# An attention-and-MLP kernel: some probability tiles turned on TensorE instead of by DMA, new numbers in the planner's table, and two rounds of planning

## The chip, the cores and the metric

The kernel runs on one NeuronCore of one Trainium2 chip. The metric is device time in microseconds (us), from launch to end; a profiled execution also has a span, from its first to its last instruction. Lower is better.

The engines are called by the names that the profile uses: PE (TensorE matmuls; PEld is its weight load), DVE (VectorE), ACT (ScalarE), POOL (GpSimd) and SP (SyncE, whose queue issues every DMA here).

## The reference

Attention over 4 batches of 8 heads, 576 tokens, 64 values a head, with scores below (row maximum minus tau) dropped, and then two MLPs over the 2304 rows that it gives.

```python
scores = scale * np.matmul(q, k.transpose(0, 1, 3, 2))
thresh = np.max(scores, axis=-1, keepdims=True) - tau
scores = np.where(scores >= thresh, scores, -1000000000.0)
attn = np.exp(scores - np.max(scores, axis=-1, keepdims=True))
attn = attn / (np.sum(attn, axis=-1, keepdims=True) + 1e-09)
x = heads_side_by_side(np.matmul(attn, v))          # 2304 x 512
x = (s * np.maximum(x @ w_in, 0) ** 2 + b) @ w_out  # 512 -> 2048 -> 512
h = x @ w2_in
out = (h / (1 + np.exp(-1.702 * h))) @ w2_out
```

## The kernel before

Nothing is issued in the order of the code. Every piece of work is handed to a `Plan` as a step with the engines that may do it, an estimated cost on each, what it reads and writes, and an urgency (`prio`). `Plan.run` lays all steps out in simulated time, on each engine the most urgent ready step first, and the kernel is then emitted in that order. Each engine works its own list strictly in that order, so a step that waits holds up all that stands behind it on its engine. The table `KN` holds the planner's numbers: `t0` to `t4` are the times from which the MLP's passes take their urgencies, `boost`, `lead` and `ahead` move attention, weight loads and weight conversions against them.

**Attention.** The heads go in 16 pairs, four to a batch, and each pair has nine score tiles of 128 rows by 576 keys, 144 tiles in all (`tile_step`). One tile runs like this: PE writes the scores S into PSUM; DVE takes the row maximum `nm` (L511), then two one-column values from it, `nb` (L522) and the threshold `tb` (L516); ACT does the exponential e (L529); DVE multiplies by the threshold mask and sums (L533, called the product below); ACT makes a half-precision copy `p` (L324), POOL the rest that the copy lost (L542 and L543); and a transposing DMA on SP's queue puts both into `PT`, `PTm` for the tile that both heads share (L545). When a pair's nine tiles are through, PE multiplies `PT` with the values V (L605, L646). Tiles named `gt`, `xa`, `xb`, `acca` and `accb` are lent to attention while the MLP does not use them yet. S has two PSUM buffers and one lent; the PSUM tag T has one and one lent, and serves V's scales, the reciprocals, and the results of L605 and L646.

**V's scales** (`prep_v`) take a reduction, six small DVE instructions (L447, L448, L449, each once for either head) and a reciprocal.

**Weights.** They arrive as 8-byte numbers in 64 blocks and are converted to 4-byte floats (`convert`): two ACT instructions (L732, L757), three on DVE (`ww` L738, `wa` L742, `wh` or `ww` L749) and a POOL addition (L759); the result is also stored.

**MLP.** Rows go in five blocks: four of 512 tokens (xa and xb) and one of 256. `hidden` (L788) multiplies by the first matrix, `project` (L851) by the second, on PE, three products for each because operands are split into a high and a low part; the first block of the first MLP does one full-precision product instead. The first MLP block needs the four pairs of batch 0.

Of the kernel before, what the change touches and what calls it, by code (L numbers as in the profile page):

```python
# [20 lines left out]
P = 128  # L21
# [23 lines left out]
    "spread": 8,  # L45
}

# [22 lines left out]
class Plan:  # L70
# [50 lines left out]
    def run(self, engines):  # L121
        steps = self.steps
        for op in steps:
            op["left"] = len(op["after"])
            for a in op["after"]:
                steps[a]["then"].append(op["n"])
        slots = {k: q[0].bufs for k, q in self.turns.items()}
        next_turn = dict.fromkeys(self.turns, 0)
# [3 lines left out]
        clock = Clock()  # L132
        for seg in range(self.segment + 1):
# [7 lines left out]
            while count < len(todo):  # L141
# [4 lines left out]
                while ends and ends[0][0] <= now:  # L146
                    for b in steps[heapq.heappop(ends)[1]]["bufs"]:
                        b.users -= 1
                        if b.users == 0:
                            slots[id(b.pool), b.tag] += 1  # L150
                moved = False
                for e in engines:
# [3 lines left out]
                    while ready[e]:  # L156
# [12 lines left out]
                        need = {}  # L169
                        ok = True  # L170
                        new = sorted((b for b in op["bufs"] if not b.live), key=lambda b: b.turn)
                        for b in new:
                            k = (id(b.pool), b.tag)
                            i = need.get(k, 0)
                            if b.turn != next_turn[k] + i or slots[k] <= i:
                                ok = False
                                break
                            need[k] = i + 1
                        if not ok:
                            put.append((p, n))  # L180
                            continue
                        for b in new:
                            b.live = True
                        for k, i in need.items():
                            next_turn[k] += i
                            slots[k] -= i
                        op["start"], op["on"] = now, e
# [7 lines left out]
                        if op["queued"]:  # L195
                            moved_at = max(now + op["queued"], moved_at)
                            if op["turns"]:
                                avail[e] = moved_at + 110.0
                            moved_at += lag
                            end = moved_at + 900.0  # L200
                        heapq.heappush(ends, (end + 180.0, n))
# [80 lines left out]
class Kernel:  # L282
# [9 lines left out]
    def consts(self, pool):  # L292
        nc = self.nc
        self.ident = pool.tile([P, P], F32, name="ident")
        make_identity(nc, self.ident)
        sc = pool.tile([P, 3], F32, name="scal")
        for i, src in enumerate((self.tau, self.s, self.b)):
            nc.sync.dma_start(sc[:, i : i + 1], src.partition_broadcast(P))
        self.s_ap, self.b_ap = sc[:, 1:2], sc[:, 2:3]
# [9 lines left out]
        self.under = pool.tile([P, 1], F32, name="under")  # L309
        nc.vector.tensor_tensor(self.under, t1, t2, ALU.add)  # L310
# [44 lines left out]
    def ps(self, tag, shape):  # L355
# [5 lines left out]
        return Buf(self.pa if own else self.px, tag, shape, F32, n if own else more)  # L361
# [55 lines left out]
    def prep_v(self, p):  # L417
# [24 lines left out]

        def scales(_):
            nc.vector.tensor_reduce(vm.ap, T.ap, AX.X, ALU.max)
# [6 lines left out]
        add({"DVE": 1085.0}, scales, [T], [vm, vs, vcol])  # L451
# [11 lines left out]
    def tile_step(self, p, i):  # L463
# [38 lines left out]
        else:  # L502
# [4 lines left out]
        tb = self.at("tb", [P, 1], F32, bufs=4)  # L507
# [3 lines left out]
            {"DVE": 668.0}, lambda _: nc.vector.tensor_reduce(nm.ap, Sv(), AX.XY, ALU.max, negate=True), [Sp], [nm],  # L511
# [6 lines left out]
        )  # L518
        nb = self.at("nb", [P, 1], F32, bufs=4)
        add(  # L520
            {"DVE": 130.0},
            lambda _: nc.vector.tensor_scalar(nb.ap, nm.ap, LOG_SP, None, ALU.add), [nm], [nb],  # L522
            prio=self.plan.prio - KN["tb"] * pace - 1.0,
# [5 lines left out]
            lambda _: nc.scalar.activation(ev(), Sv(), AF.Exp, bias=nb.ap, scale=1.0), [Sp, nb], [e],  # L529
# [4 lines left out]
                ev(), Sv(), tb.ap, ev(), ALU.is_ge, ALU.mult, accum_out=p["acc"][:, i, 0:1]  # L534
            ),
            [Sp, tb, e], [e, (p["acc"], i)], prio=self.plan.prio - KN["sc"] * pace,
# [8 lines left out]
        add({"SP": (1360.0, 1800.0, 1280.0)}, lambda _: nc.sync.dma_start_transpose(pt(), p16.ap), [p16], [(PT, part)], turns=True)  # L545
# [116 lines left out]
    def attention(self, pairs):  # L662
# [3 lines left out]
        for n, p in enumerate(pairs):  # L666
# [8 lines left out]
            if n == 0:  # L675
                do(self.prep_qk, p, 0)
            p["PT"] = {}
# [414 lines left out]
```

## Time and profile before

| | |
|---|---|
| median of 3 runs | 1100.98 us (1099.6 to 1103.26) |
| the profiled execution's own time | 1097.05 us |
| its span | 1095.2 us |
| PE busy | 1034.4 us (94%) |
| DVE busy | 810.4 us (74%) |
| ACT busy | 675.6 us (62%) |
| POOL busy | 430.6 us (39%) |

The profiled execution ran 3.9 us under the median. "Busy" is the time in which an engine had at least one instruction in work; the granted clock of PE is told apart from it, and a busy PE at half the clock does half the work.

### The profile page before, as it was taken

The page shows a single profiled execution, that of the slowest core. Times are in us where ns is not written, and L with a number is a line of the kernel's source. Part 1 is how long each engine was busy: PE and PEld are TensorE (multiplying, and loading weights), DVE is VectorE, ACT ScalarE, POOL GpSimd, SP SyncE. Part 2 cuts the span into 40 slices and gives each one's busy share as a digit, 9 for nine tenths or more (in the row PEclk, how much of TensorE's full clock was granted, in tenths as well). Part 3 has the DMA queues.
Part 4 walks back from the last instruction along what each step waited for, and adds up shares of the span by engine and source line. Part 5 has one row for each costly group of instructions (what it writes and reads, how often), then busy time and mean ns, then how long its engine had stood idle before and what let it go on. Part 6 is the DMA issues. An engine that isn't in the chain of part 4 may idle for free.

```text
span 1095.2 us, 16161 instructions
## 1 busy us (share of the span) xinstructions
PE 1034.4 (94%) x5264; PEld 754.5 (69%) x5264; DVE 810.4 (74%) x1727; ACT 675.6 (62%) x1216; POOL 430.6 (39%) x477
## 2 busy tenths in 40 slices
PE   3777889999999999999999999999999999999998
PEld 1333334445678777878877787868888888888886
DVE  6999798999898988999998878765444544444443
ACT  5776778778988765776666587655655433223221
POOL 2765565757775577556556343500000000000000
PEclk7777899999999998999999999999999999999999
DMA  7999899898988656768576866542211112020102
GB/s 220 202 188 225 217 244 247 211 255 239 227 197 227 165 136 171 204 170 223 139 187 162 198 171 145 127 139 78 78 60 66 30 49 68 1 68 10 54 34 67
DMA packets 228756, 161.54 MB, mean 147 GB/s; under 512 B 180728, under 2 KB 181312, under 8 KB 228672
## 3 DMA queue, kind: packets, MB, share of 16 engines
q1 hardware_dynamic: 228672, 160.52, 57.3%
q8 instruction: 41, 0.67, 0.3%
q14 instruction: 43, 0.35, 0.1%
HBM read 93.85 MB, written 24.15 MB: 108 GB/s over the span
## 4 chain that ended last, share of the span: by engine, by line
PE 56%; DVE 6%; issue 2%; ACT 1%; DMA 1%; SPq 0%; POOL 0%; DVEq 0%; ACTq 0%; POOLq 0%
PE y L851 27%; PE y L788 26%; PE S L490 2%; PE T L605 1%; DVE e L533 1%; DVE ww L749 1%; DVE nm L511 1%; DVE gl L339 1%; DVE ww L738 0%; DVE wl L339 0%; DMA wst<-in_moe_w_in 0%; DVE accb L864 0%; DVE wa L742 0%; DMA raw<-in_q 0%; DVE gt L816 0%
## 5 line engine op out<-in xcount | busy, mean ns | idle before, releaser
L542 POOL TENSOR_TENSOR p<-e,p 128x512 f16<-128x512 f32 x123 | 151.3, 1230 | 150.7 <-ACT p L324 122.1
L788 PE MATMUL y<-xa,wh 128*128 128x512 f32 x512 | 183.8, 453 | 0.0
L788 PE MATMUL y<-xb,wh 128*128 128x512 f32 x512 | 164.0, 401 | 0.4 <-DVE xb L339 0.4
L851 PE MATMUL y<-gh,wh 128*128 128x512 f32 (+1 forms) x384 | 156.1, 449 | 3.3 <-POOL wh L759 2.0
L529 ACT ACTIVATE e<-S,nb 128x576 f32<-128x576 f32 x144 | 104.3, 733 | 46.0 <-DVE tb L516 19.9
L533 DVE SCALAR_TENSOR_TENSOR e<-S,tb,e 128x576 f32<-128x576 f32 x144 | 115.8, 808 | 15.3 <-ACT e L529 14.3
L788 PEld LDWEIGHTS y<-xa,wh 128*128 128x128 f32 x512 | 94.0, 190 | 43.4 <-issue 26.7
L851 PE MATMUL y<-wh,gh 128*128 128x512 f32 x288 | 115.6, 401 | 3.7 <-DVE gt L816 3.7
L511 DVE TENSOR_REDUCE nm<-S 128x1 f32<-128x576 f32 x144 | 106.4, 745 | 14.5 <-PE S L497 8.0
L851 PE MATMUL y<-wl,gh 128*128 128x512 f32 x288 | 114.4, 397 | 0.0
L851 PE MATMUL y<-wh,gl 128*128 128x512 f32 x288 | 114.3, 397 | 0.0
L813 ACT ACTIVATE gt<-y 128x512 f32<-128x512 f32 (+1 forms) x80 | 44.2, 553 | 111.1 <-PE y L788 111.0
L339 DVE TENSOR_TENSOR gl<-gt,gh 128x512 fp32r<-128x512 f32 (+1 forms) x134 | 99.4, 757 | 17.7 <-ACT gh L324 17.0
L788 PEld LDWEIGHTS y<-xb,wh 128*128 128x128 f32 x512 | 94.9, 189 | 24.5 <-DVE xb L339 1.3
L816 DVE SCALAR_TENSOR_TENSOR gt<-gt,y 128x512 f32<-128x512 f32 (+1 forms) x80 | 50.4, 630 | 75.7 <-ACT gt L813 75.7
L788 PE MATMUL y<-xb,wl 128*128 128x512 f32 x256 | 101.6, 397 | 0.0
L324 ACT ACTIVATE p<-e 128x576 f16<-128x576 f32 x123 | 82.8, 678 | 30.5 <-DVE e L533 20.7
L339 POOL TENSOR_TENSOR gl<-gt,gh 128x512 fp32r<-128x512 f32 (+1 forms) x10 | 11.9, 1190 | 222.0 <-DVE gh L320 220.8
L851 PEld LDWEIGHTS y<-gh,wh 128*128 128x128 f32 x384 | 70.7, 189 | 37.1 <-issue 23.2
L851 PE MATMUL y<-gl,wh 128*128 128x512 f32 (+1 forms) x256 | 93.8, 366 | 0.5 <-POOL gl L339 0.5
L851 PE MATMUL y<-gh,wl 128*128 128x512 f32 (+1 forms) x256 | 93.8, 366 | 0.0
L324 ACT ACTIVATE wh<-wl 128x512 fp32r<-128x512 f32 x104 | 64.1, 626 | 33.6 <-DMA wl<-wd 32.2
(138 smaller groups left out, 2193.1 us busy)
## 6 DMA issues: line engine op xcount, KB each, us to landing
wl<-wd SPq DMA_DIRECT2D x128, 256.0 KB, 2.9
wst<-in_moe_w_in SPq DMA_DIRECT2D x32, 512.0 KB, 4.7
wst<-in_moe_w_out SPq DMA_DIRECT2D x32, 512.0 KB, 5.0
wd<-wh SPq DMA_DIRECT2D x32, 256.0 KB, 4.2
wd<-ww SPq DMA_DIRECT2D x32, 256.0 KB, 2.1
raw<-in_k SPq DMA_DIRECT2D x16, 288.0 KB, 3.1
raw<-in_q SPq DMA_DIRECT2D x16, 288.0 KB, 3.0
rv<-in_v SPq DMA_DIRECT2D x14, 320.0 KB, 5.5
```

The source lines that it names most:

```text
L324: nc.scalar.activation(dst(), src(), AF.Copy)
L339: engines, lambda e: self.eng[e].tensor_tensor(dst(), a(), b(), ALU.subtract), reads, writes, **kw
L490: nc.tensor.matmul(Sp[:, half, :HALF], q[h][j][:, qcols[h]], k[h][:, half * HALF : (half + 1) * HALF], start=(h, j) == (heads[0][0], 0), s ...
L511: {"DVE": 668.0}, lambda _: nc.vector.tensor_reduce(nm.ap, Sv(), AX.XY, ALU.max, negate=True), [Sp], [nm],
L529: lambda _: nc.scalar.activation(ev(), Sv(), AF.Exp, bias=nb.ap, scale=1.0), [Sp, nb], [e],
L533: lambda _: nc.vector.scalar_tensor_tensor(ev(), Sv(), tb.ap, ev(), ALU.is_ge, ALU.mult, accum_out=p["acc"][:, i, 0:1]),
L542: nc.gpsimd.tensor_tensor(p16[:, S + H2 :], e[:, :MAIN], p16[:, :MAIN], ALU.subtract)
L605: nc.tensor.matmul(Up[h * H2 : (h + 1) * H2, :], V[:, h, slot, :], p["PT"][h][:, j, :], start=start, stop=stop)
L788: nc.tensor.matmul(hp(), wt[:, kk * P : (kk + 1) * P], xv(j, kk), start=(i == 0), stop=(i == len(terms) - 1))
L813: add({"ACT": act(n, True)}, lambda _: nc.scalar.activation(t(), hp(), AF.Tanh, scale=0.851), [hps], [gt])
L816: lambda _: nc.vector.scalar_tensor_tensor(t(), t(), 1.0, hp(), ALU.add, ALU.mult), [hps, gt], [gt],
L851: nc.tensor.matmul(yp(), a, b, start=(i == 0), stop=(i == len(terms) - 1))
```

## The change

Six things are edited together.

1. For the first four head pairs (batch 0), tiles 1, 8 and 6 of each pair are no longer turned by DMA. PE transposes their nine 128x128 blocks (L614), five into one PSUM tile T and four into another, and ACT copies both to `PT` (the helper's line, now L381). These are 12 tiles, 108 PE transposes and 24 ACT copies.
2. `nb` and `tb` become one DVE instruction of three columns (L580): the scores are produced negated (the factor `qs` has its sign turned), so one addition of `nm` to the constants `both` gives the exponential's bias and the threshold.
3. Of V's scales, both heads go in one DVE instruction at a time, and the two copies to `vcol` go to POOL (L514).
4. At the start, the loads of s and b are issued behind the first pair's loads, and a one-column exponential `warm` (L347) is written ahead of the attention's first ACT step.
5. `KN` has new numbers.
6. `Plan.run` may lay the plan out twice. After the first round each step's urgency is moved a fifth of the way (`back`) to the latest start that the first round allows (`late`); the round with the smaller simulated length is kept.

```diff
 KN = {
-    "lead": 6, "boost": 30, "mix": 14, "ahead": 10, "t0": 59.94, "t1": 186.71, "t2": 461.81, "t3":
-    562.63, "t4": 650, "late": 7.58, "p5": 2.14, "p6": 3.17, "b0": 14.39, "xl": 30, "direct": 16, "c0":
+    "lead": 2, "boost": 45, "mix": 14, "ahead": 4, "t0": 54.67, "t1": 225.99, "t2": 430.13, "t3":
+    579.96, "t4": 638.63, "late": 7.31, "p5": 2.32, "p6": 3.06, "b0": 13.52, "xl": 10, "direct": 16,
...
+    "turns": 1, "tn": 4, "rounds": 2, "back": 0.2, "spread": 8,
 }
+TURNS = ((), (1, 8, 6), (0, 2, 8, 5, 7), (8,), (1, 6))
...
     def run(self, engines):
+        steps, best = self.steps, None
...
+        for i in range(KN["rounds"]):
...
+            order = self.lay(engines)
+            if best is None or self.span < best[0]:
+                best = self.span, order, [op["on"] for op in steps]
+            self.late()
...
+    def late(self):
...
+            end = min([late[m] - self.HOP.get((e, self.steps[m]["on"]), 160.0) for m in op["then"]] + [self.span])
+            length = op["end"] - op["start"]
+            t = min(end - length, last.get(e, self.span) - op["took"])
+            late[op["n"]] = last[e] = t
+        for op in self.steps:
+            op["prio"] += KN["back"] * (late[op["n"]] - op["prio"])
...
-        for i, src in enumerate((self.tau, self.s, self.b)):
-            nc.sync.dma_start(sc[:, i : i + 1], src.partition_broadcast(P))
+        nc.sync.dma_start(sc[:, :1], self.tau.partition_broadcast(P))
+        self.warm = pool.tile([P, 1], F32, name="warm")
+        nc.scalar.activation(self.warm, self.ident[:, :1], AF.Exp)
...
-        nc.vector.tensor_scalar(self.qs, z, 1.0 / math.sqrt(D), None, ALU.mult)
+        nc.vector.tensor_scalar(self.qs, z, -1.0 / math.sqrt(D), None, ALU.mult)
...
-            for h in range(2):
-                m, rows = vm[:, h : h + 1], slice(h * H2, (h + 1) * H2)
-                nc.vector.tensor_scalar(m, m, 2.0 ** -113 / unit, unit, ALU.max, ALU.mult)
-                nc.vector.tensor_scalar(m.bitcast(I32), m.bitcast(I32), 0x7F800000, None, ALU.bitwise_and)
-                nc.vector.tensor_copy(vcol[rows], m[rows])
-            nc.vector.reciprocal(vs.ap, vm.ap)
+            m = vm.ap.bitcast(I32)
+            nc.vector.tensor_scalar(vm.ap, vm.ap, 2.0 ** -113 / unit, unit, ALU.max, ALU.mult)
+            nc.vector.tensor_scalar(m, m, 0x7F800000, None, ALU.bitwise_and)
+            nc.vector.reciprocal(vs.ap, vm.ap)
+        add({"DVE": 450.0}, scales, [vm], [vm, vs])
+        def col(e):
...
+        add({"POOL": 300.0}, col, [vm], [vcol])
...
-            {"DVE": 130.0},
-            lambda _: nc.vector.tensor_scalar(tb.ap, nm.ap, -1.0, self.under, ALU.mult, ALU.subtract), [nm], [tb],
+            {"DVE": 150.0},
+            lambda _: nc.vector.tensor_scalar(nb.ap, self.both, nm.ap, None, ALU.add), [nm], [nb],
...
-        add({"SP": (1360.0, 1800.0, 1280.0)}, lambda _: nc.sync.dma_start_transpose(pt(), p16.ap), [p16], [(PT, part)], turns=True)
+        if i not in p["turns"]:
...
+            return
+        for some in (range(KS), range(KS, R)):
+            T = self.ps("T", [P, KS, P], F16)
+            def turn(_, some=some, T=T):
+                for j in some:
+                    nc.tensor.transpose(T[:, j - some[0], :], p16[:, j * P : (j + 1) * P], self.ident16)
+            add({"PE": (len(some) * 60.0 + 100.0, 60.0)}, turn, [p16], [T])
+            self.copy(
+                lambda some=some: pt()[:, some[0] : some[-1] + 1], lambda some=some, T=T: T[:, : len(some)], [T],
+                [(PT, (part, some[0]))], len(some) * P, psum=True, also=0,
+            )
...
+                plan.add({"SP": 1040.0}, lambda _: self.layer_consts(), prio=1.0)
...
+                "turns": TURNS[KN["turns"]] if b * NP + hp < KN["tn"] else (),
```

What the planner makes of it is seen at three places. On PE, in the first pair's middle and the second's start, this stood before (S are score tiles, mx and ri the small turns of V's scales and of the reciprocals):

```order
L497 MATMUL S<-kk,qb 128x288 x8
L497 MATMUL S<-kk,qa 128x288 x6
L580 MATMUL T<-ident,ri 64x128 x8
L584 MATMUL T<-ident,ri 128x128
L497 MATMUL S<-kk,qa 128x288 x2
```

And this is what stands there now; the pair of rows with p (or with `gt`, the tile lent for it) comes nine times for each tile that PE turns:

```order
L614 LDWEIGHTS p_214
L614 MATMUL T<-ident_75,p_214 128x128
L561 MATMUL S<-kk,qb 128x288 x6
L561 MATMUL S<-kk,qa 128x288 x2
L614 LDWEIGHTS gt
L614 MATMUL T<-ident_75,gt 128x128
```

The turns stand between score tiles on PE's list, so a turn whose p is not ready yet holds the next score tile back.

On DVE, around the fourth `xa` (the last step before the first MLP block has its input), this stood before:

```order
L742 TENSOR_SCALAR wa<-ww 128x65x8
L738 TENSOR_SCALAR ww<-wa 128x520
L533 SCALAR_TENSOR_TENSOR e,acc<-S,tb,e 128x576
L623 SCALAR_TENSOR_TENSOR xa<-T,vcol,rs 128x512
L533 SCALAR_TENSOR_TENSOR e,acc<-S,tb,e 128x576
L511 TENSOR_REDUCE nm<-S 128x1
L742 TENSOR_SCALAR wa<-ww 128x65x8
L522 TENSOR_SCALAR nb<-nm 128x1
L516 TENSOR_SCALAR tb<-nm,under 128x1
L749 SCALAR_TENSOR_TENSOR wh_1390<-wst,wa 128x512
```

And this stands there now:

```order
L521 SCALAR_TENSOR_TENSOR V<-rv,vs,V 128x320 x2
L697 SCALAR_TENSOR_TENSOR xa<-T,vcol,rs 128x512
L575 TENSOR_REDUCE nm<-S 128x1
L580 TENSOR_SCALAR nb<-both,nm 128x3
L575 TENSOR_REDUCE nm<-S 128x1
L580 TENSOR_SCALAR nb<-both,nm 128x3
L591 SCALAR_TENSOR_TENSOR e,acc<-S,nb,e 128x576
L489 TENSOR_REDUCE mx<-rv 128x2
L591 SCALAR_TENSOR_TENSOR e,acc<-S,nb,e 128x576
L825 SCALAR_TENSOR_TENSOR wh_1506<-wst,wa 128x512
```

Weight conversions have moved to earlier places on DVE's list, and one `nb` stands for `nb` and `tb`. From the 7th to the 36th product the lists hold 2 `ww`, 2 `wa` and 1 `wh` before, and 5, 6 and 4 now; from the 37th to the 48th, 7, 7 and 9 before, and 3, 3 and 3 now.

ACT's list began like this before:

```order
L379 ACT_TABLE_LOAD
L379 ACTIVATE kk<-kk,qs 128x576 x2
L529 ACTIVATE e<-S,nb 128x576 x2
L324 ACTIVATE p_182<-e 128x576
L326 ACTIVATE V<-rv,vs 128x320 x2
```

It now begins like this:

```order
L436 ACT_TABLE_LOAD
L436 ACTIVATE kk<-kk,qs 128x576
L347 ACTIVATE warm<-ident 128x1
L436 ACTIVATE kk<-kk,qs 128x576
L587 ACTIVATE e<-S,nb 128x576 x2
```

The table load still stands at the first `kk`, and `warm` behind it.

Written with one round of planning in place of two, the changed kernel has the same rows in the same order on all five engines: the first round is the one that is kept.

## Rows read from the trace of the kernel before

**Rows 1.** The page: busy time of the engines, share of the span.
```profile
PE 1034.4 (94%) x5264; PEld 754.5 (69%) x5264; DVE 810.4 (74%) x1727; ACT 675.6 (62%) x1216; POOL 430.6 (39%) x477
```
**Rows 2.** Busy time by stretch, cut at the 6th, 36th, 48th, 60th and last product.
```profile
core 0: us, PE busy (x) PEld busy (x) DVE busy (x) ACT busy (x) POOL busy (x), PEclk, DMA share, GB/s
26.50:93.30 66.80, 48.60 (x331) 23.62 (x333) 63.94 (x198) 49.98 (x84) 42.99 (x61) 0.76 0.95 199
93.30:143.10 49.80, 43.03 (x174) 18.38 (x172) 42.35 (x114) 38.55 (x73) 30.89 (x37) 0.81 0.91 231
143.10:199.60 56.50, 55.60 (x264) 23.48 (x263) 48.69 (x115) 44.36 (x88) 31.53 (x36) 0.98 0.95 240
199.60:705.40 505.80, 494.26 (x2500) 365.08 (x2499) 457.78 (x939) 367.75 (x661) 307.59 (x317) 0.99 0.74 187
705.40:1095.20 389.80, 383.56 (x1965) 319.39 (x1963) 180.88 (x318) 160.14 (x291) 9.47 (x11) 1.00 0.19 58
```
**Rows 3.** Waits from 26.5 to 93.3 us: total, times, longest.
```profile
PE S L497 <- DVE e L533: 11.3, 10, 2.1
ACT e L529 <- DVE tb L516: 8.6, 8, 3.4
```
**Rows 4.** Timeline of the start: start, length, engine, line, what, idle before.
```profile
0.72 0.40 SPq L298 DMA_DIRECT2D scal<-in_tau  x1
...
2.12 0.43 SPq L343 DMA_DIRECT2D kk<-in_k  x1
...
6.49 1.28 ACT L379 ACT_TABLE_LOAD   x1 [6.49 <-DMA kk<-in_k]
...
8.61 3.25 PE L497 MATMUL S<-kk,qa 64*128 64x288 f32 x12 [8.61 <-ACT kk L379]
...
12.36 0.15 DVE L522 TENSOR_SCALAR nb<-nm 128x1 f32<-128x1 f32 x1
12.43 0.20 DVE L516 TENSOR_SCALAR tb<-nm,under 128x1 f32<-128x1 f32 x1
12.55 0.81 DVE L533 SCALAR_TENSOR_TENSOR e<-S,tb,e 128x576 f32<-128x576 f32 x1
```
**Rows 5.** Groups from 0 to 108 us: V's small steps (busy, mean ns, idle before).
```profile
L448 DVE TENSOR_SCALAR vm<-vm 128x1 int32<-128x1 int32 x10 | 1.5, 154 | 0.3
L449 DVE COPY vcol<-vm 64x1 f32<-64x1 f32 x10 | 1.5, 148 | 0.3
```
**Rows 6.** Groups from 93.3 to 143.1 us: the conversion's steps, and a wait for weights.
```profile
L749 DVE SCALAR_TENSOR_TENSOR wh<-wst,wa 128x512 int32<-128x512 int32 x9 | 7.9, 882 | 0.0
...
L738 DVE TENSOR_SCALAR ww<-wa 128x520 f32<-128x520 f32 x8 | 5.5, 687 | 0.0
...
L757 ACT ACTIVATE wst<-wst 128x512 int32<-128x512 uint32 x7 | 4.6, 669 | 0.0
...
L851 PE MATMUL y<-gh,wh 128*128 128x512 f32 x4 | 3.2, 893 | 2.0 <-POOL wh L759 2.0
```
**Rows 7.** Groups from 26.5 to 93.3 us: ACT copies, SBUF source and PSUM source.
```profile
L324 ACT ACTIVATE gt<-e 128x576 f16<-128x576 f32 x18 | 12.1, 679 | 2.8 <-DVE e L533 2.5
...
L324 ACT ACTIVATE rs<-T 64x512 f32<-64x512 f32 x6 | 3.5, 588 | 0.4 <-PE T L580 0.3
```
**Rows 8.** Timeline of PE: small matmuls in groups.
```profile
33.09 1.91 PE L580 MATMUL T<-ident,ri 128*64 128x128 f32 x8
...
37.31 0.63 PE L646 MATMUL T<-PTm,V 128*64 128x64 f16 x28
```
**Rows 9.** Timeline of PE from 100 us: one half of a first-block group.
```profile
107.30 1.96 PE L788 MATMUL y<-xa,wh 128*128 128x512 f32 x4
```
**Rows 10.** Busy time in two stretches of the middle (columns as in rows 2).
```profile
350.00:450.00 100.00, 96.02 (x507) 75.20 (x506) 89.94 (x180) 69.66 (x130) 66.36 (x62) 0.97 0.67 174
...
550.00:650.00 100.00, 95.85 (x515) 76.54 (x512) 87.64 (x181) 65.07 (x109) 53.25 (x58) 1.00 0.76 180
```
**Rows 11.** DMA issues: median us from issue to landing.
```profile
PT<-p SPq DMA_TRANSPOSE x107, 3.5
```

More of the change, by code (lines that the diff above doesn't have):

```diff
@@ L121, in run, with lay @@
     def run(self, engines):
+        steps, best = self.steps, None
+        users = [(b, b.users) for b in self.bufs]
+        for i in range(KN["rounds"]):
+            for b, n in users:
+                b.users, b.live = n, False
+            for op in steps:
+                for key in ("start", "on", "t"):
+                    op.pop(key, None)
+                op["then"] = []
+            order = self.lay(engines)
+            if best is None or self.span < best[0]:
+                best = self.span, order, [op["on"] for op in steps]
+            self.late()
+        self.span, order, on = best
+        for op, e in zip(steps, on):
+            op["on"] = e
+        return order
+    def late(self):
+        last, late = {}, {}
+        for op in sorted(self.steps, key=lambda op: (-op["start"], -op["n"])):
+            e = op["on"]
+            end = min([late[m] - self.HOP.get((e, self.steps[m]["on"]), 160.0) for m in op["then"]] + [self.span])
[4 more added lines that the diff above has]
+            op["prio"] += KN["back"] * (late[op["n"]] - op["prio"])
+    def lay(self, engines):
         steps = self.steps
@@ L126, in run @@
                 steps[a]["then"].append(op["n"])
+            op["keys"] = [((id(b.pool), b.tag), b) for b in sorted(op["bufs"], key=lambda b: b.turn)]
         slots = {k: q[0].bufs for k, q in self.turns.items()}
+        blocked = {k: [] for k in slots}
         next_turn = dict.fromkeys(self.turns, 0)
@@ L132, in run, with again @@
         clock = Clock()
+        def again(k):
+            for e, p, n in blocked[k]:
+                heapq.heappush(ready[e], (p, n))
+            blocked[k].clear()
         for seg in range(self.segment + 1):
@@ L146, in run @@
                 while ends and ends[0][0] <= now:
-                    for b in steps[heapq.heappop(ends)[1]]["bufs"]:
+                    for k, b in steps[heapq.heappop(ends)[1]]["keys"]:
                         b.users -= 1
                         if b.users == 0:
-                            slots[id(b.pool), b.tag] += 1
+                            slots[k] += 1
+                            again(k)
                 moved = False
@@ L168, in run @@
                                 continue
[L169 to L173, printed above, removed]
+                        need, stuck = {}, None
+                        for k, b in op["keys"]:
+                            if b.live:
+                                continue
                             i = need.get(k, 0)
                             if b.turn != next_turn[k] + i or slots[k] <= i:
-                                ok = False
+                                stuck = k
                                 break
                             need[k] = i + 1
-                        if not ok:
-                            put.append((p, n))
+                        if stuck:
+                            blocked[stuck].append((e, p, n))
                             continue
-                        for b in new:
+                        for k, b in op["keys"]:
                             b.live = True
@@ L200, in run @@
                             end = moved_at + 900.0
+                        op["end"], op["took"] = end, avail[e] - now
                         heapq.heappush(ends, (end + 180.0, n))
@@ L308, in consts, with layer_consts @@
         nc.vector.tensor_scalar(t2, sc[:, 0:1], 0.0, None, ALU.max)
-        self.under = pool.tile([P, 1], F32, name="under")
-        nc.vector.tensor_tensor(self.under, t1, t2, ALU.add)
+        self.both = pool.tile([P, 3], F32, name="both")
+        nc.vector.memset(self.both, 0.0)
+        nc.vector.tensor_scalar(self.both[:, 0:1], t2, 0.0, LOG_SP, ALU.mult, ALU.add)
+        nc.vector.tensor_tensor(self.both[:, 1:2], t1, t2, ALU.add)
+    def layer_consts(self):
+        for i, src in enumerate((self.s, self.b)):
+            self.nc.sync.dma_start(self.sc[:, i + 1 : i + 2], src.partition_broadcast(P))
     def copy(self, dst, src, reads, writes, cols, scale=None, psum=False, also=0, **kw):
@@ L360, in ps @@
         own = i % (n + more) < n
-        return Buf(self.pa if own else self.px, tag, shape, F32, n if own else more)
+        return Buf(self.pa if own else self.px, tag, shape, dt, n if own else more)
     def prep_qk(self, p):
@@ L544, in tile_step @@
         add({"POOL": Shared(pool(MAIN) + pool(H2))}, low, [e, (p16, 0)], [(p16, 1)])
-        add({"SP": (1360.0, 1800.0, 1280.0)}, lambda _: nc.sync.dma_start_transpose(pt(), p16.ap), [p16], [(PT, part)], turns=True)
+        if i not in p["turns"]:
+            add(
+                {"SP": (1360.0, 1800.0, 1280.0)}, lambda _: nc.sync.dma_start_transpose(pt(), p16.ap), [p16], [(PT, part)],
+                turns=True,
+            )
+            return
[8 more added lines that the diff above has]
+                [(PT, (part, some[0]))], len(some) * P, psum=True, also=0,
+            )
     def finish_sums(self, p):
```

30 lines of the change are left out of this document (14 added, 16 removed), and 4 rows, old and new, of the table KN.

## The prediction

> **What bounds the kernel now.** I read the page first, then busy time cut into stretches, then the waits and groups inside the stretches. The page says that PE is the scarce engine: 94% busy, DVE 74%, ACT 62% [rows 1]. A share over the whole span hides where the rest goes, so I cut the span at the 6th, 36th, 48th, 60th and 144th product, which are places that both orders have [rows 2]. The reader is to see five different stretches there.
>
> From 26.5 to 93.3 us (30 score tiles of batch 0, no MLP yet) DVE is busy for 63.94 of 66.8 us, ACT for 49.98 and PE for 48.60 at a mean granted clock of 0.76. PE's score tiles wait for DVE's products, 11.3 us in ten waits, while ACT's exponentials wait for `tb` [rows 3]: DVE sets the pace. From 93.3 to 143.1 us no engine is full: PE 43.03 of 49.8 us at a clock of 0.81, DVE 42.35, ACT 38.55. From 143.1 to 199.6 us PE is busy for 55.60 of 56.5 us, and from there to the last product for 494.26 of 505.8 us, at clocks of 0.98 and 0.99. Behind it 389.8 us of MLP remain with PE 383.56 us busy at full clock [rows 2]. So the time is PE's work plus what is lost before 143 us, plus 11.5 us of idle PE in the middle. The change adds work to PE and can save only what is lost.
>
> **The change part by part.** The sum is made against the profiled execution, 1097.05 us (span 1095.2); it lies 3.9 us under the median of the runs, and I add that at the end.
>
> *Start.* The load of the first `kk` is issued at 2.12 us, behind three loads that begin at 0.72 [rows 4], so each takes 0.47 us of SP's queue; two of them move behind it: -0.9 us. The table load of 1.28 us follows that load and stays in front of the first score tile, because in the new order `warm` stands behind `kk`, not ahead. If the load lands no earlier it is 0; if the table load were hidden, 0.9 + 1.28 = 2.2 us would go. I take -0.9.
>
> *First stretch, DVE.* Where `nb` and `tb` begin at 12.36 and 12.43 and the next product at 12.55 [rows 4], one instruction for two saves 0.07 us (if what follows keeps its 0.12) to 0.12; for 30 tiles -2.1 (to -3.6). V's scales lose one each of two small steps and two copies, 2 x 0.154 + 2 x 0.148 = 0.6 us [rows 5], -1.8 for three pairs. The copies that go to POOL are hidden: POOL has 24 us free in this stretch [rows 2]. But the list now has 3 `ww`, 4 `wa` and 3 `wh` more: 7 x 0.687 + 3 x 0.882 = +7.5, pricing `wa` as `ww` [rows 6]. DVE: 63.9 - 2.1 - 1.8 + 7.5 = 67.5.
>
> *First stretch, ACT.* Ten of the twelve turned tiles fall here. Each adds two copies out of PSUM, of 640 and 512 columns. No row has such a copy of half-precision numbers; the nearest, 512 columns from PSUM, takes 588 ns [rows 7], which gives 0.66 us as a mean, +13.2. Eight more ACT steps of the conversion at 0.669 [rows 6] are +5.4, two more copies to p at 0.679 [rows 7] +1.4. ACT: 49.98 + 20.0 = 70. The engine that had 17 us to spare becomes the fullest. With the idle time that DVE has now (2.9 us) the stretch takes some 72 us: +5. Its lower bound is DVE alone, 67.5, about +1; the upper one is ACT waiting as long for DVE as now, 70 + 8.6 = 78.6, +12.
>
> *First stretch, PE and DMA.* Nothing in the trace is a half-precision 128x128 turn. From below: 28 matmuls of half precision with 64 columns take 0.63 us, 0.022 each; from above: 8 full-precision turns take 1.91, 0.24 each [rows 8]. I take 0.1, nearer to the first, whose operands have the same type. Ten tiles of nine blocks add 9 us (2 to 22): 48.6 + 9 = 57.6 of 72, hidden behind ACT and DVE. Ten transposing DMAs of 3.5 us to land [rows 11] leave a queue that is 0.95 busy [rows 2]; no engine's time hangs on them while DVE sets the pace: 0. If that cover went, PE's turns would cost their 9 us.
>
> [...]
>
> *Second and third stretch.* From the 37th to the 48th product DVE loses 4 `ww`, 4 `wa` and 6 `wh`, 8 x 0.687 + 6 x 0.882 = 10.8 us, and with 13 `tb` and two sets of scales some 12.9: 42.35 to 29.5. ACT loses eight conversion steps, 5.4: 33. The wait of PE for weights, 2.0 us [rows 6], should go with them. For PE: a mean clock of 0.81 between full and half means 0.38 of the time at half, so the busy 43.03 us hold 0.38 x 43.03 / 2 = 8.2 us of slowness, and 6.8 are idle. The new order also has 16 first-block matmuls before the 48th tile instead of 20; two take 1.96 us [rows 9], 3.9 less. Full-clock work is then 43.03 - 8.2 - 3.9 = 30.9 us. Filled to 86%, as now (43.03/49.8), the stretch takes 36: -13.8, of which 3.9 is work put off: -10 for the two stretches. The most that can come back is 6.8 + 8.2 and the third stretch's 0.9 + 1.1 = 17; the least is 0.
>
> *The middle.* Attention tiles are spread thinner: between the 96th and the 120th tile the new order has 690 MLP matmuls instead of 546, and between the 120th and the 144th fewer. DVE has 90 of 100 us to do in the stretches where PE idles 4 us each [rows 10], and 84 x 0.07 + 9 x 0.6 = 11 us less over all 505.8. But thinner here is denser there: -1, with -8 to +8.
>
> *The tail*, with PE full, has the same matmuls: 0. *The second round of planning* changes no row: 0.
>
> Sum: -0.9 + 5 - 10 - 1 = -6.9 us, 1090.2 for the profiled execution, and with 3.9 about **1094 us** as a median.
>
> **The rivals.**
> *A larger gain, about 1085.* The first stretch costs 1, since ACT's and DVE's waits overlap, and the middle gives back half its 11.5 idle us: -0.9 + 1 - 10 - 6 = -16. For it: DVE's fullness where PE idles [rows 10]. Against: three engines above 80% in one stretch with orders fixed.
> *Nothing, about 1100.* The first stretch takes its 10 to 12 us, because each turned tile now passes ACT four times, and what the second gains only pays it. For it: ACT at 70 of 72. Against: conversions done there aren't done later.
> *Slower, about 1109: PE's turns hold the score tiles back.* PE's list is in order, and a turn waits for POOL's half of p. Score tiles wait up to 2.1 us now [rows 3]; if each of 12 turned tiles delays the next score tile so, 25 us of waiting falls on a stretch that DVE and ACT already fill, of which I let 10 hide behind PSUM's three score buffers: 15 + 5 - 0.9 - 10 - 1 = +8. It decides from about 12 us of such waits on. 0.24 us for a block would do it too: 48.6 + 22 = 70.6 us of PE at its present clock. [...]
> *The change doesn't do what it says.* For `warm` and the second round the order shows that already; the rest of the order is new throughout, so "no change" as such is excluded.
>
> **How the numbers follow.** I give the forecast (1089 to 1097) 0.43, the larger gain 0.20, nothing 0.19, slower 0.18. With 0.3% (3.3 us) as the bound of what a measurement can tell, faster has 0.63, same 0.19, slower 0.18. The range reaches from the larger gain with some room, 1081, to short of the slow case's far side, 1106.
>
> **What would show it.** The first score tile starts 0.9 us earlier, still behind a table load. The 36th product comes 3 to 6 us later than 93.3, with ACT about as full as DVE. PE's turns take near 0.1 us a block. The 60th product comes about 6 us earlier than 199.6 with two pairs of first-block matmuls more done, and PE's clock before 143 us is higher than 0.81. PE's idle time from the 60th to the last product stays near 11.5 us. It would be wrong if DVE or ACT idle over 10 us in the first stretch, or if the middle's idle time doubles.

## The result and the profile after

The changed kernel takes 1107.15 us (median; 1105.6 to 1108.09) against 1101.36 of the kernel before in the same comparison: a ratio of 1.0051, 95% interval 1.003 to 1.0072. It is slower by half a per cent, where 1094 was forecast. The profiled execution took 1108.09 us with a span of 1106.3, so 11.1 us more span than before.

The page, busy line, beside [rows 1]:

```profile
PE 1044.0 (94%) x5372; PEld 765.5 (69%) x5372; DVE 833.9 (75%) x1516; ACT 684.0 (62%) x1233; POOL 455.2 (41%) x523
```

DVE has 211 instructions fewer than before and is busy for 23.5 us more. That one row contradicts the forecast, in which DVE's work shrank over the whole span.

Busy time by stretch, cut at the same products as [rows 2] (after the start's own row):

```profile
core 0: us, PE busy (x) PEld busy (x) DVE busy (x) ACT busy (x) POOL busy (x), PEclk, DMA share, GB/s
0.00:24.20 24.20, 10.08 (x47) 5.05 (x47) 16.29 (x43) 15.21 (x26) 7.06 (x19) 0.86 0.74 240
24.20:103.60 79.40, 59.88 (x425) 33.24 (x423) 73.46 (x170) 64.77 (x115) 49.59 (x73) 0.72 0.73 162
103.60:142.10 38.50, 35.32 (x202) 17.57 (x201) 33.02 (x78) 31.68 (x58) 20.67 (x31) 0.92 0.79 178
142.10:203.70 61.60, 59.53 (x247) 24.98 (x245) 52.31 (x96) 48.12 (x93) 39.47 (x44) 1.00 0.88 229
203.70:717.20 513.50, 496.59 (x2510) 365.58 (x2509) 480.37 (x820) 365.78 (x658) 331.07 (x350) 1.00 0.75 187
717.20:1106.30 389.10, 382.63 (x1949) 319.06 (x1948) 178.50 (x321) 158.42 (x287) 7.39 (x9) 1.00 0.19 57
```

Against [rows 2] the start gives 2.3 us, the first stretch costs 12.6, the second and third together give 6.2, the middle costs 7.7 and the tail gives 0.7: +11.1 in all. The forecast was -0.9, +5, -10, -1 and 0. In the first stretch DVE is busy for 73.46 us where 67.5 was forecast. In the middle, with 119 instructions fewer than before, it is busy for 480.37 instead of 457.78 us.

Which DVE instructions grew is read from the groups of the whole span, kept apart by shape (busy, mean ns of one, idle before):

```profile
L580 DVE TENSOR_SCALAR nb<-both,nm 128x3 f32<-128x3 f32 x144 | 63.4, 448 | 0.9
L507 DVE TENSOR_SCALAR vm<-vm 128x2 int32<-128x2 int32 x16 | 6.8, 425 | 0.6
L506 DVE TENSOR_SCALAR vm<-vm 128x2 f32<-128x2 f32 x16 | 4.6, 286 | 0.0
```

Before, the two one-column instructions that `nb` replaces took 49.2 us in all:

```profile
L516 DVE TENSOR_SCALAR tb<-nm,under 128x1 f32<-128x1 f32 x144 | 28.7, 201 | 0.0
L522 DVE TENSOR_SCALAR nb<-nm 128x1 f32<-128x1 f32 x144 | 20.5, 142 | 0.6
```

The fused one takes 63.4. The view of the tile tells why a mean is not enough (duration min/median/max in ns, then how long ACT's exponential sat idle for it, in how many waits):

```profile
L580 DVE TENSOR_SCALAR nb<-both,nm x144: 169/229/1283, 9.9 to 714.8; 128x3 f32<-128x3 f32 x144
...
  DVE nb L580: 55.8, 49
```

Most `nb` take 0.23 us, some up to 1.28, and ACT's exponentials sit idle for them 55.8 us in 49 waits. The timeline shows what a long one does:

```profile
53.22 1.16 POOL L600 TENSOR_TENSOR p<-e,p 128x512 f16<-128x512 f32 x1 [0.44 <-ACT p L381]
...
53.22 1.18 DVE L580 TENSOR_SCALAR nb<-both,nm 128x3 f32<-128x3 f32 x1
...
54.33 0.31 POOL L601 TENSOR_TENSOR p<-e,p 128x64 f16<-128x64 f32 x1
54.52 0.74 ACT L587 ACTIVATE e<-S,nb 128x576 f32<-128x576 f32 x1 [0.50 <-DVE nb L580]
54.60 1.16 POOL L600 TENSOR_TENSOR gt<-e,gt 128x512 f16<-128x512 f32 x1
...
55.31 0.47 DVE L580 TENSOR_SCALAR nb<-both,nm 128x3 f32<-128x3 f32 x1
```

The first `nb` begins with POOL's subtraction and ends 0.02 us behind it, while POOL's next instruction (54.33) is already at work: `nb` waits for one instruction, not until POOL has nothing left to do. The second begins in the middle of the next subtraction (54.60 + 1.16 = 55.76) and ends at 55.78. Of the 144, 39 take over 0.4 us, and within each of these exactly one POOL instruction ends; on average `nb` ends 26 ns later. It is the same without exception: 56 `nb` begin while POOL's instruction has 0.23 us or more to go, and each of them ends 22 to 32 ns behind that instruction. What is over 0.216 us, called the excess below, adds up to 33.5 us (the expectations below were written with 32.7): 1.8 at the start, 5.5 in the first stretch, 3.1 and 1.4 in the next two, 21.8 in the middle. V's small steps on two columns (L506, L507) behave alike, 6.2 us in all. The profile books all this as work of DVE, not as a wait, so no view of waits names POOL.

The conversion's `ww` and `wa` are one-source instructions on DVE as `nb` is. Their rows in the same view:

```profile
L814 DVE TENSOR_SCALAR ww<-wa x64: 677/684/697, 22.0 to 564.5; 128x520 f32<-128x520 f32 x64
L818 DVE TENSOR_SCALAR wa<-ww x64: 674/684/697, 27.7 to 566.3; 128x520 int32<-128x520 int32 x64
```

The longest is 697 ns, 23 over the shortest, although 40 of the one and 30 of the other begin while POOL works: these never wait for POOL.

Other instructions of DVE already waited so in the kernel before, and its trace shows it. Two of them, a one-source cast and the conversion's `wh` with two sources (min/median/max):

```profile
L320 DVE CAST wh<-wl x24: 412/427/1210, 334.4 to 916.7; 128x512 fp32r<-128x512 f32 x24
L749 DVE SCALAR_TENSOR_TENSOR wh<-wst,wa x32: 632/686/1650, 28.7 to 260.0; 128x512 int32<-128x512 int32 x32
```

Of the 64 instructions of L749, 19 are longer than 0.82 us, and each of these ends 544 to 549 ns behind the end of a POOL instruction. The same wait stood in the trace that the prediction was made from; its price for `wh`, 0.882 us, is a mean with such waits in it.

### The profile page after: what moved, and what is told of

The parts are those of the page before. It is cut to its first block, busy times and chain, and to the rows that moved or that the text cites. A ratio compares the mean times of both kernels' runs of the same rounds, so it can differ in the third digit from the quotient of the medians.

```text
span 1106.3 us, 16113 instructions
## 1 busy us (share of the span) xinstructions
PE 1044.0 (94%) x5372; PEld 765.5 (69%) x5372; DVE 833.9 (75%) x1516; ACT 684.0 (62%) x1233; POOL 455.2 (41%) x523
## 4 chain that ended last, share of the span: by engine, by line
PE 60%; DVE 23%; ACT 5%; issue 4%; DMA 4%; POOL 2%; SPq 0%; ACTq 0%; POOLq 0%; DVEq 0%
PE y L927 26%; PE y L864 26%; DVE e L591 4%; DVE nm L575 4%; DVE nb L580 3%; PE S L561 2%; PE T L679 2%; PE S L554 2%; DVE gl L396 1%; DVE kk L455 1%; DMA wst<-in_moe_w_out 1%; DVE ww L814 1%; DMA wl<-wd 1%; PE T L654 1%; DMA PT<-p 1%
## 5 line engine op out<-in xcount | busy, mean ns | idle before, releaser
L600 POOL TENSOR_TENSOR p<-e,p 128x512 f16<-128x512 f32 x123 | 153.8, 1251 | 135.3 <-ACT p L381 98.5
L396 POOL TENSOR_TENSOR gl<-gt,gh 128x512 fp32r<-128x512 f32 (+1 forms) x19 | 25.2, 1330 | 361.9 <-DVE gh L377 355.8
L587 ACT ACTIVATE e<-S,nb 128x576 f32<-128x576 f32 x144 | 105.9, 737 | 77.2 <-DVE nb L580 55.8
L591 DVE SCALAR_TENSOR_TENSOR e<-S,nb,e 128x576 f32<-128x576 f32 x144 | 115.9, 808 | 14.2 <-ACT e L587 14.1
L864 PEld LDWEIGHTS y<-xa,wh 128*128 128x128 f32 x512 | 93.1, 189 | 43.8 <-issue 26.1
L396 DVE TENSOR_TENSOR gl<-gt,gh 128x512 fp32r<-128x512 f32 (+1 forms) x125 | 92.5, 755 | 15.5 <-ACT gh L381 14.7
L381 ACT ACTIVATE p<-e 128x576 f16<-128x576 f32 x123 | 83.1, 677 | 20.2 <-DVE e L591 11.5
L381 ACT ACTIVATE wh<-wl 128x512 fp32r<-128x512 f32 x107 | 65.9, 625 | 34.6 <-DMA wl<-wd 34.1
```

What stands on the lines that cost most here:

```text
L381: nc.scalar.activation(dst(), src(), AF.Copy)
L396: engines, lambda e: self.eng[e].tensor_tensor(dst(), a(), b(), ALU.subtract), reads, writes, **kw
L587: lambda _: nc.scalar.activation(ev(), Sv(), AF.Exp, bias=nb[:, 0:1], scale=-1.0), [Sp, nb], [e],
L591: lambda _: nc.vector.scalar_tensor_tensor(ev(), Sv(), nb[:, 1:2], ev(), ALU.is_le, ALU.mult, accum_out=p["acc"][:, i, 0:1]),
L600: nc.gpsimd.tensor_tensor(p16[:, S + H2 :], e[:, :MAIN], p16[:, :MAIN], ALU.subtract)
L864: nc.tensor.matmul(hp(), wt[:, kk * P : (kk + 1) * P], xv(j, kk), start=(i == 0), stop=(i == len(terms) - 1))
```

## The experiments

In all of them but e5, e6, e10 and e11 the rows stand in the same order on every engine as in the kernel that is edited, but for the edited instructions. Those four were laid out anew by the planner. "Split" is short for e3, the changed kernel with one-column instructions in both places.

**Is it the three columns?** e1_nb_split writes `nb` by two one-column instructions:

```diff
-            lambda _: nc.vector.tensor_scalar(nb.ap, self.both, nm.ap, None, ALU.add), [nm], [nb],
+            for c in range(2):
+                nc.vector.tensor_scalar(nb[:, c : c + 1], self.both[:, c : c + 1], nm.ap, None, ALU.add)
```

> The changed kernel with nb written by two one-column instructions in place of one of three columns, every engine's list otherwise the same. Theory A (a DVE instruction of several dense columns waits for POOL's instruction to end): each of the two takes 0.14 to 0.20 us whatever POOL does, the 32.7 us of excess leave DVE, ACT's waits for nb fall from 55.8 to under 30 us, the first stretch shortens by 4 to 8 us and the middle by 4 to 9; total 1092 to 1098. Rival B (the time is lost to ACT's and PE's added work in the first stretch and to the tighter order, and the waits of nb are covered): 1105 to 1109, unchanged within 3 us.

Measured: 1096.07 us, ratio to the kernel before 0.9967 (0.995 to 0.9984). One more instruction per tile makes the kernel 9 us faster by the ratios (0.9967 for 1.0051), 11 by the times. The middle is 9.1 us shorter (504.4), the first stretch only 2.9 (76.5), less than I expected. ACT still waits 48.6 us for `nb` in this run, so the expected fall below 30 was wrong: the total of these waits does not tell what the wait for POOL costs.

e3_nb_vm_split does the same to `nb` and gives V's steps L506 and L507 one instruction for each head again.

> The split nb, and V's two small steps split into one column for each head again (their excess was 6.2 us). Theory A: 1 to 4 us under the split nb alone. Rival B: within 2 us of the changed kernel, or slower by the 32 added instructions (about 4 us of DVE).

Measured: 1094.5 us, 0.9946 (0.9924 to 0.9967), a span of 1089.0. V's steps take 142 and 149 ns and none of the `nb` over 0.216 us. The 1.6 us to e1 lie within the intervals.

**Does the fused instruction do it alone?** e4_before_nb3 takes the kernel before, with its own order and its `tb`, and only makes `nb` three columns wide:

```diff
-        nb = self.at("nb", [P, 1], F32, bufs=4)
+        nb = self.at("nb", [P, 3], F32, bufs=4)
...
-            lambda _: nc.vector.tensor_scalar(nb.ap, nm.ap, LOG_SP, None, ALU.add), [nm], [nb],
+            lambda _: nc.vector.tensor_scalar(nb.ap, self.three, nm.ap, None, ALU.add), [nm], [nb],
```

> The kernel before with its nb made three dense columns wide and nothing else: the same number of instructions, the same lists. Theory A: nb's mean goes from 0.14 to 0.4 us or more, 25 to 35 us of excess on DVE, and the time rises by 8 to 15 us, 1109 to 1116. Rival B: nb takes 0.17 us and the time stays within 3 us of 1101.

Measured: 1126.89 us, 1.0244 (1.0222 to 1.0266), a loss of 27 us, twice what was expected. The groups of its DVE:

```profile
L524 DVE TENSOR_SCALAR nb<-three,nm 128x3 f32<-128x3 f32 x144 | 70.0, 486 | 0.6
L518 DVE TENSOR_SCALAR tb<-nm,under 128x1 f32<-128x1 f32 x144 | 28.9, 201 | 0.0
```

Two columns that nobody reads cost 486 instead of 142 ns a tile, and `tb`, one column and just behind, stays at 201. The excess of `nb` is 39 us.

**Is it that the columns lie side by side?** e2_nb_strided gives every column a gap (`[P, 3, 2]`, of which `[:, :, 0]` is used, in source and result).

> The changed kernel with nb still one instruction of three columns, but every second element of its tiles is used, so that the columns are not dense. Theory A: if dense columns are what waits for POOL, nb takes about 0.2 us always and the time is that of the split nb or 1 to 3 us less (one instruction fewer a tile), 1090 to 1097. If three columns wait however they lie, the excess stays above 25 us and the time at 1107. Rival B: 1104 to 1109 either way.

Measured: 1106.3 us, 1.0067 (1.0044 to 1.0089), mean of `nb` 437 ns, excess 32.0 us. It waits as in the changed kernel; density has no part.

**Is it the length of POOL's instruction?** e8_pool_halves cuts POOL's 512-column subtraction in the changed kernel into two of 256 columns, so that POOL comes free twice as often.

> The changed kernel with the fused three-column nb kept, and POOL's 512-column subtraction for p cut into two of 256 columns, about 0.65 us each in place of 1.25, at some 0.1 us more of POOL's time for a tile. If nb waits for the end of the POOL instruction at work, its excess falls from 32.7 to 16 to 20 us and its longest from 1.28 to about 0.75; the total falls by 3 to 7 us, to 1100 to 1104. If nb only waits for a POOL queue to drain, excess and time stay as they are or grow.

Measured: 1106.18 us, 1.0061 (1.0041 to 1.0081). The groups of POOL and of DVE:

```profile
L602 POOL TENSOR_TENSOR p<-e,p 128x256 f16<-128x256 f32 x246 | 180.7, 755 | 122.9 <-ACT p L381 87.3 <-issue 25.5 <-POOL p L603 2.4
...
L580 DVE TENSOR_SCALAR nb<-both,nm 128x3 f32<-128x3 f32 x144 | 63.3, 447 | 0.9
```

My expectation failed, for the excess (16 to 20 us; it is 33.3) and for the time. Excess and time stay, as I had expected if `nb` waits until POOL's queue is empty; that reading fails by the timeline, since here too each of the 67 `nb` that begin with 0.23 us or more of a POOL instruction to go ends 22 to 32 ns behind that one instruction, most of them with POOL's next one at work. Among the `nb` over 0.3 us, one held by such a piece waits for about half as long (334 instead of 606 ns), but 36 are held by them instead of 24: a piece of 755 ns is more than half of 1251, and POOL is busy for 481.2 us instead of 455.2. Other POOL instructions hold about as many as in the changed kernel.

**Is it the shape?** e9_nb_rows is the split kernel with `nb` written as two rows of two columns at pitch 3, the way `ww` and `wa` are addressed in rows.

> The kernel with V's small steps in one column each, and nb again one instruction, but over two rows of two columns whose tiles have a pitch of three, so that the pattern has two free dimensions; ww and wa, 520 columns in rows of 8 at a pitch of 9, never waited for POOL. If the shape of the pattern decides, nb takes about 0.23 us always, the excess is under 3 us, and the time is 0 to 4 us under the kernel with nb split, 1090 to 1095. If any instruction of more than one column of this size waits, the excess is again 30 us and the time near 1105.

Measured: 1104.02 us, 1.0035 (1.0022 to 1.0049), mean 437 ns, excess 31.9 us: rows as such don't spare the wait.

What was left is the pair of counts, the source's and the result's. The `nb` and V's steps that waited so far have the same count in both; `ww` goes from 65 rows to one run of 520. e12_nb_odd does that with `nb`: three rows of two columns in, one run of six out, counts of 3 and 6. e13_nb_even is the same with four rows, counts of 4 and 8. Both are the split kernel otherwise:

```diff
+        self.both = pool.tile([P, 3, 3], F32, name="both")
+        nb = self.at("nb", [P, 6], F32, bufs=4)
...
+            lambda _: nc.vector.tensor_scalar(nb.ap, self.both[:, :, :2], nm.ap, None, ALU.add), [nm], [nb],
```

> As the kernel with split nb and split V steps (1094.5 us), except that nb is again one instruction, over six columns: the constants lie in three rows of two at pitch 3, the result is one run of six. Source and result so have outermost counts of 3 and 6, odd and unequal, as the 128x520 conversion steps have 65 and 520, which never waited for POOL. [...] Rival B, that any few-column instruction of this kind waits: mean 0.43 to 0.47 us, over 25 nb longer than 0.4 us, and the time 1101 to 1108 us, as with two rows of two (1104.0).

> The control of the run beside it: four rows of two in, a run of eight out, so counts of 4 and 8, both even. [...] If rows in and one run out are what spares the wait, whatever the counts: mean 0.21 to 0.26 us and 1089 to 1097 us as its neighbour. [...]

Measured on one chip: 1087.41 us for counts of 3 and 6, ratio 0.9885 (0.9864 to 0.9905); 1102.68 for 4 and 8, ratio 1.0026 (1.0012 to 1.004). The group of the first:

```profile
L584 DVE TENSOR_SCALAR nb<-both,nm 128x6 f32<-128x6 f32 x144 | 29.2, 210 | 0.9
```

Its row in the view of the tile:

```profile
L584 DVE TENSOR_SCALAR nb<-both,nm x144: 157/210/221, 9.8 to 692.0; 128x6 f32<-128x6 f32 x144
```

The group of the second:

```profile
L584 DVE TENSOR_SCALAR nb<-both,nm 128x8 f32<-128x8 f32 x144 | 63.8, 451 | 0.9
```

And its row in the view of the tile:

```profile
L584 DVE TENSOR_SCALAR nb<-both,nm x144: 169/231/1324, 9.8 to 709.7; 128x8 f32<-128x8 f32 x144
```

Six columns never take more than 221 ns, though 89 of the 144 begin while POOL works; eight take up to 1324, with 38 over 0.4 us. I had expected 1089 to 1097 us of the first and 1101 to 1108 of the second if the pair of counts decides; the time with six columns is 1.6 us below that. That any few-column instruction of this kind waits is excluded by the first run, and by the second that rows in and one run out spare the wait whatever the counts: what differs between the two is the counts alone. Of `nb`, V's small steps, the cast, `ww` and `wa`, those with counts of 3 and 3 (mean 448 ns), 2 and 2 (286 and 425 in V's steps, 437 in e9), 4 and 8 (451) and 512 and 512 (the cast, up to 1210) wait; those with 3 and 6 (at most 221) and with 65 and 520 (at most 697) don't. No run shows why these pairs differ, or what other pairs would do. Nor does one show why the cast of 512 columns, where it doesn't wait, takes some 427 ns (its median) and `ww` and `wa` with 520 take 684.

**Is it the turns, the table of numbers, the table load?** e5_no_turns is the split kernel with `turns` 0, e6_old_numbers with the `KN` of before, e10_old_no_turns with both.

> The split kernel (nb and V's small steps in one column each), with every tile turned by DMA again and one round of planning, which is the round that the split kernel keeps; the plan is made anew. If PE's turns are what the first stretch gains from (relief of the DMA queue), 3 to 8 us slower than the split kernel, 1097 to 1103. If the 24 ACT copies cost more than the relief brings (the prediction's first stretch, +5), 2 to 6 us faster, 1088 to 1093, with ACT under 52 us busy between the 6th and the 36th product.

> The split kernel with the old table of numbers and the turns kept. The prediction puts the gain of the second stretch (-10) down to weight conversions moved ahead by the new table: then 5 to 10 us slower than the split kernel, 1099 to 1105. Rival: the gain comes from the cheaper small steps and from the turns, whatever the table: within 3 us of 1094.

> The split kernel with the old table of numbers and no turns: it differs from the kernel before by the small DVE steps, the later loads of s and b and the planner's costs for them. If those parts alone help, 1 to 5 us under before, 1095 to 1099. If the new plan's order matters more than they do, anywhere from 1093 to 1106.

Measured: 1103.21 us (1.0025, 1.0011 to 1.0039), 1112.25 (1.0118, 1.0093 to 1.0142) and 1115.14 (1.013, 1.0114 to 1.0146), all slower than the split kernel; e6 and e10 lie outside of everything that I had expected. Without turns (e5) the 36th product comes at 93.1 us instead of 98.9, so the plan with turns is 5.8 us later there, but the time is lost later, between the 60th and the last product (510 us against 501). e10 has the table of before and no turns, and yet it is 15 us slower than the kernel before. How far that speaks for turns or table is what e11_nudged asks: the split kernel with `t1` moved by one microsecond (225.99 to 226.99), which shifts a few hundred rows.

> The split kernel with one number of the table moved by 1 us (t1 from 225.99 to 226.99), one round of planning: no step changes its cost, but the lists are laid out anew and differ in a few hundred places. If the gain lies in the mechanisms that the prediction names, within 3 us of the split kernel's 1094.5. If it lies as much in how the plan happens to fall, 4 us or more away, up to 1104.

Measured: 1104.49 us, 1.0031 (1.0018 to 1.0045). It runs as the split kernel does up to about the 90th product and then loses 10 us. One stretch of it:

```profile
550.00:650.00 100.00, 93.95 (x503) 74.73 (x504) 81.29 (x168) 61.69 (x105) 49.82 (x58) 0.98 0.64 166
```

The same stretch of the split kernel:

```profile
550.00:650.00 100.00, 98.17 (x535) 78.77 (x534) 87.92 (x177) 66.33 (x111) 56.50 (x65) 1.00 0.68 175
```

So where the plan happens to fall is worth some ten microseconds by itself, as much as all that e5 loses. These three runs settle neither what the turns nor what the table are worth.

e7_warm_first writes `warm` as ACT's first step of the plan, so that the table load doesn't wait behind `kk`:

> The split kernel with the one-column exponential made ACT's first step of the plan, so that the table load stands ahead of kk's wait; every other list the same. If the start is on the path, the first score tile starts 1.3 us earlier, at 5.8 us, and the total is 1 to 1.5 us under the split kernel, 1093. Rival: the first tiles wait for the second head's loads or DVE anyway, and the total doesn't move (1094.5).

Measured: 1093.83 us, 0.9941 (0.9918 to 0.9963), the split kernel's time within the intervals. Its start:

```profile
0.71 1.28 ACT L756 ACT_TABLE_LOAD   x1 [0.71 <-PEq L1161]
...
5.77 3.23 PE L564 MATMUL S<-kk,qa 64*128 64x288 f32 x12 [5.77 <-ACT kk L435]
```

The first score tile is 1.2 us earlier than in the split kernel (7.00), and the first product ends at 11.9 us in both: the table load was not on the path.

## Why the prediction was wrong

**The step that failed** is "First stretch, DVE": "one instruction for two saves 0.07 us [...] to 0.12". It prices a three-column instruction by the rows of one-column ones [rows 4], and these are of another kind: none of them waits for POOL, though 90 of the 144 of each start while POOL works (the longest take 156 and 213 ns). The fused one costs 448 ns on average, so a tile pays 0.1 us more and not 0.1 less. "V's scales" failed by the same rule. What it led to is the excess: 33.5 us of `nb` and 6.2 of V's steps, 21.8 of it in the middle, where the prediction had 11 us less of DVE's work. The same paragraph says of POOL only that it has 24 us free. I let the copies that go to POOL cost nothing for that reason, without asking what POOL's work does to DVE.

The traces show the two kinds side by side: counts of 3 and 3, 2 and 2, 4 and 8 wait (means of 286 to 486 ns), counts of 3 and 6 and of 65 and 520 don't (longest 221 and 697 ns), though no view shows why. The trace of before had no instruction like the fused one, but it had the cast of 512 columns, which waited: its median is 427 ns, and each of the four over 430 ns ends 281 to 284 ns behind the end of a POOL instruction. A price of a DVE instruction with an operand pattern that no row shows was thus open on the side of a loss, and I gave it bounds of 0.07 and 0.12, both gains.

**With that one step put right, the sum comes within 3.1 us, and each of its terms within 2.5.** The six-column kernel, e12, is what the change was meant to be, except for V's steps, which are split. Its stretches, in us, with the forecast's terms (cut at the same products; differences to [rows 2]):

| stretch | forecast | changed kernel | split (e3) | six columns (e12) |
|---|---|---|---|---|
| to the 6th product | -0.9 | -2.3 | -2.7 | -3.1 |
| 6th to 36th | +5 | +12.6 | +8.3 | +3.9 |
| 36th to 60th | -10 | -6.2 | -7.5 | -8.2 |
| 60th to 144th | -1 | +7.7 | -4.6 | -3.5 |
| behind | 0 | -0.7 | +0.3 | +0.9 |
| sum | -6.9 | +11.1 | -6.2 | -10.0 |

Two rows of e12's stretches, the first and the middle:

```profile
23.40:94.10 70.70, 50.60 (x425) 31.09 (x423) 68.06 (x174) 63.60 (x114) 49.57 (x73) 0.87 0.84 182
...
192.20:694.50 502.30, 492.61 (x2510) 365.52 (x2509) 458.50 (x838) 366.74 (x658) 330.42 (x350) 1.00 0.75 191
```

DVE's forecast of 67.5 us meets 68.06. That the stretch's 72 meets 70.70 is luck: the 72 was ACT's 70 and 2.9 us of idle time (72.9, in fact), and ACT is busy for 63.60 us. What sets the stretch is DVE, with 68.06 us and 2.6 idle. The changed kernel has the same instructions on PE there (x425), at a clock of 0.72 instead of 0.87, which makes PE's busy time 59.88 instead of 50.60 us: the changed kernel's trace has two levels, 0.50 and 1.00, and nine of PE's turns take 1.14 us at the one (from 54.72 us on) and 0.68 at the other (from 40.43). PE is idle for about as long in both (19.5 and 20.1 us); why it was granted the lower level for more of the stretch no run tells. The four executions of the changed kernel, at mean clocks of 0.971 to 0.988, differ by 2.5 us, so the clock is no large part of the loss. In the middle PE idles 16.9 us with the wait and 9.7 without, against 11.5 before: the bounds of -8 and +8 held, and DVE's fullness where PE idles [rows 10] was the right reason to look there, for a loss as for a gain.

**Other steps.**
- Start: -0.9 was forecast, -2.3 measured. `kk` is issued at 1.19 instead of 2.12 us as worked out, and the table load stays in front, as the order of ACT's list said; the load landed 1.52 us earlier than in [rows 4], not 0.93, and the first score tile with it:

```profile
1.19 0.41 SPq L400 DMA_DIRECT2D kk<-in_k  x1
...
4.97 1.28 ACT L436 ACT_TABLE_LOAD   x1 [4.97 <-DMA kk<-in_k]
...
7.09 3.25 PE L561 MATMUL S<-kk,qa 64*128 64x288 f32 x12 [7.09 <-ACT kk L436]
```

- PE's turns: 0.1 us a block was right, and the ACT copy's 0.66 us as a mean of two sizes was near (0.64). Groups of the first stretch, ten tiles with 90 blocks in 9.7 us:

```profile
L614 PE MATMUL T<-ident,gt 128*128 128x128 f16 x54 | 6.1, 265 | 2.1 <-POOL gt L601 1.0 <-DVE xm L728 0.8 <-DVE xa L697 0.3
L614 PE MATMUL T<-ident,p 128*128 128x128 f16 x36 | 3.6, 266 | 0.0
L381 ACT ACTIVATE PT<-T 128x640 f16<-128x640 f16 x5 | 3.5, 692 | 0.6 <-PE T L614 0.6
L381 ACT ACTIVATE PT<-T 128x512 f16<-128x512 f16 x5 | 3.0, 591 | 0.0
```

- In these rows a turn costs PE 9.7 us / 90 = 0.11. Their mean of 265 ns is one turn's length, while others overlap it: 54 such lengths are 14.3 us, in 6.1 us of busy time.
- ACT's 70 us in the first stretch was too much; it had 64.77, and ACT was not the fullest engine. The added lengths were right (20.0; their sum grew by 19.1), but ACT's instructions overlap a little where they stand back to back, so its busy time grew by 14.8 only. ACT idled there for 14.6 us, over the 10 that the prediction named as a sign of being wrong.
- PE's clock before 143 us was to be higher than 0.81: it was 0.72 in the first stretch and 0.92 in the second.
- The 36th product came 10.3 us later than before, not 3 to 6, and the 60th 4.1 us later, not 6 earlier. The second stretch shrank to 38.5 us, near the forecast (36); the third grew by 5.1, where 3.9 of work put off was forecast.
- The slower rival gave 1109, near to the result, by another mechanism: PE's turns holding the score tiles back. PE idled 2.1 us in front of its turns in the first stretch, not 25, and e12 has every turn and is the fastest kernel. The score tiles' waits for DVE's products, 11.3 us before [rows 3], are 13.2 in the changed kernel and 9.0 in e12.
- The two points where the change does nothing (`warm`, the second round) were right.

**What stays open.** What the turns and the new table are worth: each laid-out plan differs, and e11 shows that a plan's chance is worth 10 us. For the same reason part of the split and six-column kernels' gain over the kernel before may be the table's fit to this very order; only comparisons within one order (the changed kernel, e1, e2, e3, e8, e9, e12, e13) are free of it. Nor does a run tell why e4 lost 27 us on 39 us of excess, where the changed kernel pays 18 to 20 against e12 (by the ratios, by the times) on 33.5 + 6.2.

## What to carry to other kernels

Before fusing small one-source DVE instructions, look at the counts of the fused one: with 3 and 3, 2 and 2 or 4 and 8 in source and result, it waited for the instruction that POOL had at work (means of 286 to 486 ns), and with POOL 41% busy `nb` cost more than the two instructions that it replaced (63.4 us for 49.2). One column (at most 217 ns), or three rows in and one run of six out (at most 221), didn't wait, and the second keeps the fusion's gain: here 15 us lay between two forms of one instruction (e12 and e13, 1087.41 and 1102.68 us). And an engine that has fewer instructions and more busy time than before (here DVE, 211 fewer and 23.5 us more) may be waiting inside its instructions; read min, median and max, not the waits, and read them in the trace of before too.

## What the hardware showed that I had not expected

An instruction of three columns took up to 1.28 us because POOL was at work, and one of 520 columns (684 ns) never waited. Two columns more that nobody reads cost the kernel before 27 us. A microsecond's change of one planner number, with no step's cost changed, cost some 10 us.
